# A new instruction list for the first half of a fused conv and gMLP kernel, with normalizations allowed on GpSimd

## The chip, the core and the metric

The kernel runs on one core of one Trainium2 chip. The metric is device microseconds of one execution. A core has five engines with a queue of instructions each, which run in order: PE (TensorE, matmuls and transposes by identity), DVE (VectorE), ACT (ScalarE), POOL (GpSimd), and SP (SyncE), which here only issues transfers. They wait for each other by semaphores. PE's results land in PSUM, and DVE and ACT read them from there.

## What is computed

With S = 2048 positions and D = 640 channels, in bfloat16:

```python
sa, ca, ga, sb, cb, gb = split(silu(c) @ w_mod, 6)
h = layernorm(x) * (1 + ca) + sa
kv = shift_conv(k, 4 taps) * v                      # (S, D)
y = irfft(rfft(pad(kv)) * rfft(pad(ssm_k)))[:S] + kv * ssm_D   # long convolution along S
x = x + ga * (h * y)
h = layernorm(x) * (1 + cb) + sb
z = gelu(h @ w_in)                                  # (S, 2 * 864)
z1, z2 = z[:, :864], layernorm(z[:, 864:])
x = x + gb * ((z1 * (w_sp @ z2 + b_sp)) @ w_out)
```

## The kernel before

The channels are cut into 5 units of 128, the positions into 16 tiles of 128. A group is 4 tiles.

**Convolution, for each unit.** SP loads k and v transposed (line L513), PE forms the four taps with diagonal matrices (`taps`), DVE multiplies by v (`tv`, L545), the product goes to a scratch in HBM (`kvw`, L551) and is read back in the layout of the Fourier step (`ldX`, L382, which also loads ssm_k, `X<-in_A_ssm_k`). PE makes stage 1 of the transform (`s1`), ACT or DVE copies it to SBUF (`s1c`, L240). Then, for 8 pairs of frequencies, PE finishes the transform (`fwd`), ACT copies that of ssm_k (`khc`), DVE multiplies the two (`prod`, L454), POOL or DVE sums real and imaginary parts (`csum`, L468), PE transforms back (`inv`), ACT or DVE copies the result into Z (`zc`, L240). A unit's Z is turned by a DMA transpose (`zt`, ZT<-Z, L675; for the last unit on PE, `zfl`, with copies `zk`), PE makes the last stage (`y`, for the last unit `yl`), and DVE multiplies by the modulated h (`ym`, L668; `yml`, L730). ZT has one buffer: a unit's transpose can start only when the last `y` of the unit before has read it.

**First layernorm.** `ln1` takes the statistics of a tile of x, `rstd1` and `nmr1` give 1/sigma and -mean/sigma for 8 tiles, `xn` (L595 to L603) writes the normalized tile to gh, `ghm` (L651) multiplies and adds ca and sa. The vectors come from matmuls with w_mod, whose six parts are loaded by `ldw` (L610) through one buffer.

**Second half.** `res` (L688) adds to x, `ln2` and `ag2` take statistics, `rstd2` and `nmr2` follow, `zx` (L819 to L831) normalizes a tile. Group 0 goes in two pieces of two tiles and is turned on PE (`hfl`) and modulated out of PSUM (`hmod`, L851 and L853); groups 1 to 3 are turned by DMA (`turn`, L871) and modulated in place (`hmod2`, L873 to L880). PE multiplies by w_in (`zz`), ACT applies gelu. Up to here the order of all engines is a list written out, ORDER: each entry is an engine's letter (P, A, D, G for POOL, S) and the number of a recorded operation; the letter decides which engine does it, where the operation allows more than one, and the sequence decides the order on every engine. `fill` operations are matmuls on the identity whose result nobody reads; FILLS says how many matmuls each has. They stand in the list like the rest.

**Last part.** The mixing with w_sp (L964), the projection (L985) and the output follow in plain loops; the list doesn't reach them.

An operation names the engines that may do it, as here the first normalization:

```python
op("DA", "xn", fn, r=[("xt", (u, n)) for u in range(NU)] + [("mv1", n), ("rs1", n // 8)],
   w=[("gh", (u, n // TB)) for u in range(NU)])
```

Of the kernel before, what the change touches and what calls it, by code (L numbers as in the profile page):

```python
# [10 lines left out]
ALU = mybir.AluOpType  # L11
# [13 lines left out]
NU = 5  # L25
# [5 lines left out]
PE_FLIPS = (4,)  # L31
TB = 4
NQ = DU // 4
FILLS = (7, 2, 1, 1, 4, 3, )
MODE = ('susussus', 'susussus', 'susussus', 'susussus', 'susussus')
SLOTS = dict(Tf=2, W=2, X=3, X1=4, KH=9, T=3, Z=3, ZT=1, wm=1, big=2, dg=2, st1=2, s1=1, sm=2, pu=2, pz=2)
PSUM_TAGS = ("s1", "sm", "pu", "pz")


ORDER = """  # L40
S82 G101 A4 D0 D13 D14 A16 D100 A1 D15 D102 D109 D110 A111 D121 G5 D17 S2 G6 P1029 P8 A11 D86 A112 P1030 P7 S19 S21
P145 P148 D115 D10 D116 A118 A149 A146 A147 D23 P1031 P26 A150 A117 D18 G119 S83 D87 P1032 P151 P154 D103 P24 D122
A123 A124 G125 D27 A152 D104 G126 D25 G120 S20 A156 A106 A105 G107 G108 G113 G114 D153 S88 D90 S22 P28 D29 P30 A155
P227 A228 D31 A33 P142 D143 P167 A168 P171 A172 P139 S523 D527 P229 A230 D528 P157 S34 S32 S35 A158 G144 D140 P161
A162 P231 A232 P133 P159 A160 P169 A170 D134 P233 P136 D127 P163 A128 S84 A164 G36 S85 P165 D529 A166 G48 D530 P37
A137 D38 D129 P173 A174 D175 P176 G135 P41 A178 D177 G138 D42 A234 P179 A180 A181 P182 D183 P43 D44 S524 G141 P39 D40
A184 P185 G72 A531 A532 P195 D186 D196 S3 P9 A12 A533 P191 D192 S46 S47 P51 G187 P201 D202 D52 G188 P189 P193 A190
G197 G198 A534 A194 P211 D212 G213 P217 P199 P53 D218 P221 D222 S45 A200 P49 S526 A542 A543 S89 P205 G214 D206 G207
P203 G208 P245 A246 D54 P251 D252 D50 P215 S565 P55 D56 A544 P247 A248 P253 A254 P237 G130 G131 P568 A238 P566 A567
P249 A250 D216 P257 A258 D535 G60 S525 D204 P209 A210 D538 D539 D540 P235 S91 A236 P219 P255 A256 P241 A242 P239 G536  # L50
A240 G223 G224 P225 D93 P301 A569 D537 D541 D302 P259 D260 A545 G261 P291 D292 S570 P573 D574 P303 P571 D546 P265 A304
D266 S57 A220 A553 D549 P307 A308 S58 D572 S92 P243 A244 A226 D550 G262 P263 P65 P305 A306 G547 D548 P285 D286 P293
D551 P275 D276 G287 G288 A264 A557 P325 A326 D554 A294 P267 S59 D552 G707 G591 D612 D66 A558 P269 D270 G271 G272 P327
A328 P315 P289 A316 P63 D64 A559 P329 A330 S575 P576 D561 P309 D577 S94 P295 D296 A310 D96 A268 P578 P331 A332 P323
A324 S70 S71 D562 A563 G613 P273 D560 G595 P313 P375 D649 D579 P333 D334 A314 P67 A564 D68 G297 G298 A274 P61 D62 P319
G597 A376 A320 G598 D596 P349 D350 P77 A290 P377 A378 P343 D344 P73 P317 A555 D592 D556 D593 P379 A318 S599 P311 A312
P299 S69 G335 A380 G336 A300 P321 A322 G345 G346 P337 A338 P279 D78 P381 A382 D594 P600 G672 D74 D280 G281 D601 P79
P369 D370 P277 A278 P347 A348 P387 A388 D282 D80 P602 P383 A384 P283 D603 A284 S95 P399 A400 P604 D650 D605 G616 D617
P365 P359 P351 A352 P606 D366 D607 G371 G372 D360 G709 P401 A402 S97 D99 P395 A396 D676 P75 P403 A404 P353 D354 P385
A386 D614 D76 G655 P373 P405 G618 D619 A406 G361 G362 P363 P397 A398 S580 G355 P339 A374 P449 A450 P407 P367 A368 A364  # L60
D340 P413 P453 A454 D408 G615 D414 S620 P621 D622 P393 G609 A394 P341 A342 P451 A452 S81 D656 S98 P623 P391 A392 P439
G608 D651 G356 P357 D677 D624 P455 A358 P625 G652 A456 P389 A390 D440 P427 D626 G409 G410 P627 P411 D674 P417 P473
A474 D428 G429 A412 G430 P457 A458 D418 S657 G419 D420 P415 P433 D434 A416 P479 A480 P443 P421 A422 P471 A472 D444
P475 G653 G654 A476 P431 G435 D436 P461 A462 P423 D628 D424 P477 P437 A432 P658 D659 A478 G673 P467 A468 G629 D630
D631 P463 A464 P581 A582 G445 G446 P660 D661 G634 P481 D482 A438 P441 A442 P662 D663 P497 D498 P425 A426 P517 D518
P447 A448 G483 G484 D710 P465 A466 P664 P485 A486 D632 P507 D508 G713 P459 A460 P499 P469 G519 A470 D633 P487 G670
D665 S583 D488 A500 G520 P521 A522 P501 G509 G510 G675 P584 D502 P513 D514 G671 P511 P491 D492 G503 G504 A512 G493
A585 D494 G708 P489 A490 P515 A516 S678 P679 P505 A506 D680 P681 D682 G667 P495 G666 P683 D638 D684 A496 P719 D720
P721 A722 P685 D686 D687 P717 G692 D690 P715 D716 S586 P587 D691 A718 G639 D689 P723 D688 A588 D724 D725 D727 D726
D756 P589 A590 D755 P732 D728 D729 P746 D636 D731 G757 D758 A759 D760 D730 D733 D769 D768 G770 P1033 P1034 P761 D763  # L70
D765 D764 D734 D735 D738 G610 P762 A767 A766 P739 D736 D737 D771 S754 P809 P813 D635 P815 A810 S753 P781 A772 A773
A814 D637 P775 A779 D693 D831 G714 D695 D747 G711 G712 D696 A816 D833 D694 D832 A780 D834 D697 G835 D611 P774 D776
D777 D778 A782 D836 D837 D839 D838 P791 A792 D793 A840 D740 P811 A812 D644 D741 D742 D744 P788 A789 D643 P795 P805
A806 D668 D701 A796 D699 D642 P802 D700 P798 A799 A803 D641 S841 P784 D846 P821 A822 A785 P819 A820 A842 D844 P817
P823 A824 D845 D843 P877 D743 D745 D900 A878 P847 A848 P881 D640 A882 P889 A890 P850 D646 P864 A818 D698 D897 D898
D899 D786 G901 D902 D903 A906 D905 D904 A851 S907 P854 A855 D748 D751 D849 P887 D647 D749 D852 G702 D669 D706 D705
D783 A865 D703 P871 A888 P883 A884 D645 D963 D965 A872 D750 P875 A876 D648 A909 D752 P857 A858 P879 D704 A880 D964
A911 D910 P885 A886 D912 D966 D908 D807 G967 D968 P868 A869 D873 P861 A862 A969 D971 A970 D870 D972 P923 P913 A924
A914 P920 A921 P951 A952 P927 S973 D859 D797 D790 D922 P930 D794 A931 D932 D800 D915 A928 D801 P937 A938 D977 D976
A978 P947 A948 P916 P934 A917 A935 D975 P943 A944 D804 D974 P989 P996 P979 A997 A990 D929 D933 D808 D863 D787 G825  # L80
D826 A827 A980 D830 D829 D866 D867 D853 P1000 A1001 D918 P1003 A1004 D856 P1015 A1016 D919 P945 D874 D860 P982 A983
D1002 A946 D828 P1021 G891 D892 A893 D981 D991 D939 P993 D936 A994 A1022 D940 P986 D895 D1005 D925 D926 D896 A987
P1017 P1011 A1012 P953 A954 A1018 P1007 D984 D988 D992 D985 G957 D998 D894 A1008 P941 D1006 D958 A959 D961 A942 P1013
D995 A1014 P949 A950 D999 G1023 P1009 D1024 A1028 A1026 P955 A962 A956 P1019 D1025 D960 D1027 A132 A1020 A1010
"""


# [36 lines left out]
def kernel(  # L124
# [20 lines left out]
    nc = tc.nc  # L145
# [26 lines left out]
    xt = persist.tile([P, NT, D], BF16)  # L172
# [17 lines left out]
    mv2 = persist.tile([P, NT, ADIM], F32)  # L190
    rstd2 = persist.tile([P, NT], F32)
    nmr2 = persist.tile([P, NT], F32)
# [11 lines left out]
    with ExitStack() as actx:  # L204
        consta = actx.enter_context(tc.tile_pool(name="consta", bufs=1))
        gh = consta.tile([P, NT, D], BF16)
# [10 lines left out]
        mv1 = consta.tile([P, NT, ADIM], F32)  # L217
        rstd1 = consta.tile([P, NT], F32)
        nmr1 = consta.tile([P, NT], F32)
# [8 lines left out]
        op = plan.op  # L228
# [366 lines left out]
        def xn(n):  # L595
            def fn(e):
                if e is nc.scalar:
                    e.activation(gh[:, n, :], xt[:, n, :], ACT.Identity, bias=nmr1[:, n:n + 1], scale=rstd1[:, n:n + 1])
                else:
                    e.tensor_scalar(gh[:, n, :], xt[:, n, :], mv1[:, n, 0:1], rstd1[:, n:n + 1],  # L600
                                    op0=ALU.subtract, op1=ALU.mult)
            op("DA", "xn", fn, r=[("xt", (u, n)) for u in range(NU)] + [("mv1", n), ("rs1", n // 8)],
               w=[("gh", (u, n // TB)) for u in range(NU)])  # L603

        def mod(j):
# [205 lines left out]
        def norm_piece(g, p, ns, xn2):  # L811
# [7 lines left out]
            for i, n in enumerate(ns):  # L819
                first = i == 0 and p == 0  # L820

                def norm(e, n=n, first=first):
                    if first:
                        new(xn2, "Z", [P, TB, D])
                    dst = tl[xn2][:, n % TB, :]
                    if e is nc.scalar:
                        e.activation(dst, xt[:, n, :], ACT.Identity, bias=nmr2[:, n:n + 1], scale=rstd2[:, n:n + 1])  # L827
                    else:
                        e.tensor_scalar(dst, xt[:, n, :], mv2[:, n, 0:1], rstd2[:, n:n + 1], op0=ALU.subtract, op1=ALU.mult)
                op("DA", "zx", norm, r=[("mv2", n), ("rs2", (g, p)), ("nm2", (g, p))] + [("xt", (u, n)) for u in range(NU)] + ([] if first else [(xn2, "new")]),  # L830
                   w=[(xn2, n % TB)] + ([(xn2, "new")] if first else []), new=[(xn2, "Z")] if first else [])  # L831

        def flip_piece(g, p, ns, xn2, hT):
# [24 lines left out]
        def z_group(g):  # L858
# [9 lines left out]
            if g >= PE_GROUPS:  # L868
# [4 lines left out]
                for dt in range(ND):  # L873
# [3 lines left out]
                            e.activation(h, h, ACT.Identity, bias=sb_col[:, dt:dt + 1], scale=cb1_col[:, dt:dt + 1])  # L877
                        else:
                            e.tensor_scalar(h, h, cb1_col[:, dt:dt + 1], sb_col[:, dt:dt + 1], op0=ALU.mult, op1=ALU.add)
                    op("DA", "hmod2", modulate, r=["sb", "cb"], w=[(hT, (dt, 0))])  # L880
            def p_of(n):
                return [n in q for q in pieces(g)].index(True)
            tags = ("pu", "pz", "pu", "pz")
# [156 lines left out]
```

## Time and profile before

| | us |
|---|---|
| median of 6 runs | 320.87 |
| lowest and highest run | 319.0, 321.86 |
| the profiled execution, its own time | 320.26 |
| its span, first to last instruction | 318.5 |
| PE busy | 306.8 |
| DVE busy | 208.5 |
| ACT busy | 152.4 |
| POOL busy | 104.1 |

How to read it: the profile has one row for each instruction with its start and duration; groups of rows give a line of the kernel, engine, operation, tile written and tiles read, shape, count, total and mean duration, and then the engine's idle time in front of them with what ended it. In the 40 slices a digit is the busy share of a slice of 8 us in tenths. The first 16 or 17 slices are the part up to the matmuls with w_in; after it DVE, ACT and POOL have little to do. The chain of waits is followed back from the last instruction, at each step to what released it.

### The profile page before, as it was taken

The numbers are of one execution on the slowest core, as the hardware profiler recorded it, in microseconds if no ns is written. First come the engines' busy times: TensorE is split into PE (matmuls) and PEld (weight loads), VectorE is DVE, ScalarE is ACT, GpSimd is POOL, SyncE is SP. The second block draws the span as 40 slices with busy tenths as digits, with TensorE's granted clock in tenths as the row PEclk, the third lists the DMA queues.
The fourth block names the chain that finished last, engine by engine and source line by source line (L and its number), as shares of the span: only waits on it lengthen the run. The fifth ranks groups of instructions, "written<-read, shape, count | busy, mean of one in ns | idle before, by whom it ended". The sixth has DMA issues, their size and how long they took to land.

```text
span 318.5 us, 6389 instructions
## 1 busy us (share of the span) xinstructions
PE 306.8 (96%) x2574; PEld 203.2 (64%) x2574; DVE 208.5 (65%) x448; ACT 152.4 (48%) x270; POOL 104.1 (33%) x134
## 2 busy tenths in 40 slices
PE   7988999999999998999999999999999999999996
PEld 2666787877899897555555555555555555555554
DVE  7899999989899899998957961522222223332333
ACT  4989899998798655676777682000000000000001
POOL 2665464878688897722001120000000000000000
PEclk9999999999999999999999999999999999999999
DMA  8999999996966398030429307896556555522221
GB/s 148 248 241 249 247 261 252 226 218 173 239 168 134 106 201 315 2 65 18 84 56 169 59 1 166 195 214 93 141 115 118 115 115 117 115 51 49 49 51 62
DMA packets 127026, 45.00 MB, mean 141 GB/s; under 512 B 116144, under 2 KB 126229, under 8 KB 126997
## 3 DMA queue, kind: packets, MB, share of 16 engines
q1 hardware_dynamic: 126698, 44.29, 63.3%
q8 instruction: 20, 0.33, 0.4%
q10 hardware_dynamic: 298, 0.31, 0.3%
q14 instruction: 10, 0.07, 0.1%
HBM read 16.11 MB, written 5.24 MB: 67 GB/s over the span
## 4 chain that ended last, share of the span: by engine, by line
PE 75%; DMA 13%; DVE 5%; SPq 4%; POOL 1%; issue 1%; ACT 1%; DVEq 0%; POOLq 0%
PE ps L964 29%; PE pu L237 13%; PE pz L237 13%; PE po L985 9%; PE sm L237 6%; DMA X<-kv_scr 4%; DMA kv_scr<-big 4%; SPq L513 3%; PE s L237 3%; DMA ZT<-Z 3%; DMA wm<-in_w_mod_dram 2%; DVE Tf L454 2%; POOL W L468 1%; ACT Z L827 1%; SPq L382 1%
## 5 line engine op out<-in xcount | busy, mean ns | idle before, releaser
L964 PE MATMUL ps<-X,wT 128*128 128x432 bf16 x512 | 95.7, 346 | 0.0
L964 PEld LDWEIGHTS <-wT 128*128 128x128 bf16 x512 | 50.1, 98 | 42.2
L977 ACT COPY uT<-pt 128x896 bf16<-128x896 bf16 x1 | 0.9, 906 | 118.4 <-PE pt L976 118.4
L237 PEld LDWEIGHTS <-Z 128*128 128x128 bf16 x320 | 31.2, 98 | 26.9 <-DVE Z L853 0.3
L237 PE MATMUL pu<-X,M 128*128 128x128 bf16 (+1 forms) x480 | 45.3, 237 | 1.0 <-DVE Tf L454 0.9
L237 PEld LDWEIGHTS <-M 128*128 128x128 bf16 x480 | 37.2, 98 | 5.8 <-issue 1.3
L468 POOL TENSOR_TENSOR W<-Tf 128x256 bf16<-128x256 f32 x46 | 33.8, 756 | 18.9 <-DVE Tf L454 17.0
L967 DVE SCALAR_TENSOR_TENSOR u<-ps,bcol,G 128x432 bf16<-128x432 f32 x18 | 12.0, 667 | 42.3 <-PE ps L964 42.3
L985 PE MATMUL po<-w_o,uT 128*128 128x320 bf16 (+2 forms) x231 | 33.2, 295 | 0.1
L240 ACT CAST X<-s 128x1024 bf16<-128x1024 f32 x30 | 30.9, 1030 | 4.1 <-PE s L237 3.7
L237 PE MATMUL pu<-big,Z 128*128 128x432 bf16 x160 | 32.6, 346 | 0.0
L237 PE MATMUL pz<-big,Z 128*128 128x432 bf16 x160 | 32.3, 346 | 0.0
L454 DVE TENSOR_TENSOR Tf<-pu,KH 128x1024 f32<-128x1024 f32 x25 | 30.2, 1218 | 2.6 <-PE pu L237 1.4
L967 DVE SCALAR_TENSOR_TENSOR u<-ps,bcol,M 128x432 bf16<-128x432 f32 x14 | 9.3, 667 | 31.6 <-PE ps L964 31.6
L985 PEld LDWEIGHTS <-uT 128*128 128x128 bf16 (+1 forms) x231 | 22.2, 97 | 9.9 <-issue 0.2
L237 PEld LDWEIGHTS <-G 128*128 128x128 bf16 x330 | 24.9, 98 | 1.6
L240 ACT CAST Z<-pz 128x512 bf16<-128x512 f32 x38 | 22.4, 601 | 7.1 <-PE pz L237 7.0
L240 ACT CAST KH<-pu 128x512 bf16<-128x512 f32 x40 | 23.4, 602 | 2.4 <-PE pu L237 2.4
L987 DVE TENSOR_TENSOR ot<-po,xt 128x320 bf16<-128x320 f32 (+1 forms) x33 | 15.9, 482 | 12.6 <-PE po L985 12.6
L237 PEld LDWEIGHTS <-X 128*128 128x128 bf16 x288 | 17.9, 97 | 7.5 <-DMA X<-kv_scr 3.3
L237 PE MATMUL s<-F1bd,X 128*128 128x256 bf16 x128 | 19.2, 272 | 1.5 <-DMA X<-kv_scr 1.3
L237 PE MATMUL sm<-big,dg 128*128 128x512 bf16 (+1 forms) x80 | 20.1, 379 | 0.5 <-DVE dg L530 0.3
(146 smaller groups left out, 417.2 us busy)
## 6 DMA issues: line engine op xcount, KB each, us to landing
wm<-in_w_mod_dram SPq DMA_DIRECT2D x6, 800.0 KB, 5.9
xt<-in_A_q_dram SPq DMA_DIRECT2D x4, 640.0 KB, 6.4
out_dram<-ot SPq DMA_DIRECT2D x15, 160.0 KB, 2.4
big<-in_B_w_in_dram SPq DMA_DIRECT2D x2, 1080.0 KB, 9.7
X<-in_A_ssm_k_dram SPq DMA_DIRECT2D x4, 512.0 KB, 6.2
kv_scr<-big SPq DMA_DIRECT2D x4, 512.0 KB, 4.3
X<-kv_scr SPq DMA_DIRECT2D x4, 512.0 KB, 4.3
w_o<-in_B_w_out_dram SPq DMA_DIRECT2D x6, 160.0 KB, 4.5
```

What stands on the lines that cost most here:

```text
L237: nc.tensor.matmul(o, lhsT=w, rhs=x, start=start, stop=stop)
L240: (e.copy if e is nc.scalar else e.tensor_copy)(dst, src)
L382: e.dma_start(tl[name][:, cs, :], src[:, d0 // 8 + cs.start:d0 // 8 + cs.stop, :])
L454: e.tensor_tensor(T_[:], (tl[pu] if src is None else tl[src])[:, :, :, None, :].to_broadcast(shape), tl[KH][:, :, None, :, :].to_broadcast ...
L468: e.tensor_tensor(tl[W][:, :, o, :], T_[:, :, 0, o, :], T_[:, :, 1, 1 - o, :], op=ALU.add if o else ALU.subtract)
L513: e.dma_start_transpose(tl[name][:, o + h * m:o + (h + 1) * m], src[0, h * m:(h + 1) * m, dt * P:(dt + 1) * P])
L827: e.activation(dst, xt[:, n, :], ACT.Identity, bias=nmr2[:, n:n + 1], scale=rstd2[:, n:n + 1])
L964: nc.tensor.matmul(ps[:, :FC], lhsT=wTs[t][:, s_, :], rhs=tl["z2_%d" % (s_ // TB)][:, s_ % TB, fc * FC:(fc + 1) * FC], start=(s_ == 0), st ...
L967: nc.vector.scalar_tensor_tensor(u[:, sl], ps[:, :FC], bcol[:, t:t + 1], z1[t][:, sl], op0=ALU.add, op1=ALU.mult)
L977: nc.scalar.copy(uTs[t][:], pt[:])
L985: nc.tensor.matmul(ps[:, :hi - lo], lhsT=uTs[t][:fsz[ft], ft, :], rhs=w_o[:fsz[ft], ft, lo:hi], start=(ft == 0), stop=(ft == NFT - 1))
L987: nc.vector.tensor_tensor(ot[:, lo:hi], ps[:, :hi - lo], xt[:, t, lo:hi], op=ALU.add)
```

## The change

The list is replaced by another one, with 1032 entries instead of 1035 (three fills fewer). `xn`, `zx` and `hmod2` may also stand on POOL, and on POOL the two normalizations are written as x * rstd + (-mean * rstd) in place of (x - mean) * rstd. Nothing else differs. The diff without the list itself:

```diff
-FILLS = (7, 2, 1, 1, 4, 3, )
+FILLS = (9, 2, 3, )
...
 def xn(n):
...
+                elif e is nc.gpsimd:
+                    e.tensor_scalar(gh[:, n, :], xt[:, n, :], rstd1[:, n:n + 1], nmr1[:, n:n + 1], op0=ALU.mult, op1=ALU.add)
                 else:
                     e.tensor_scalar(gh[:, n, :], xt[:, n, :], mv1[:, n, 0:1], rstd1[:, n:n + 1],
                                     op0=ALU.subtract, op1=ALU.mult)
-            op("DA", "xn", fn, ...
+            op("DAG", "xn", fn, ...
...
+                    elif e is nc.gpsimd:
+                        e.tensor_scalar(dst, xt[:, n, :], rstd2[:, n:n + 1], nmr2[:, n:n + 1], op0=ALU.mult, op1=ALU.add)
...
-                op("DA", "zx", norm, ...
+                op("DAG", "zx", norm, ...
...
-                    op("DA", "hmod2", modulate, ...
+                    op("DAG", "hmod2", modulate, ...
```

The first entries of the list, before and after (0 is the identity, 82 the first load, 101 an iota, 4 a table load, 18 and 13 bits of the partition number, 100 steps of the angles):

```diff
-S82 G101 A4 D0 D13 D14 A16 D100 A1 D15 D102 D109 D110 A111 D121 G5 D17 S2 G6 P1029 P8 A11 D86 A112 P1030 P7 S19 S21
+D0 D18 D100 A4 D13 A1 S82 G101 D102 D109 D15 D110 A111 A112 D115 G5 S2 D6 D14 A16 P1029 P8 D11 D86 P7 A10 A23 D17
```

Operations by engine where the lists differ in number:

| operation | before | after |
|---|---|---|
| xn, 16 | DVE 9, ACT 7 | DVE 2, ACT 3, POOL 11 |
| zx, 16 | DVE 9, ACT 7 | DVE 8, ACT 3, POOL 5 |
| hmod2, 15 | DVE 11, ACT 4 | DVE 4, ACT 3, POOL 8 |
| s1c, 48 | DVE 6, ACT 42 | DVE 9, ACT 39 |
| zc, 40 | DVE 2, ACT 38 | DVE 4, ACT 36 |
| zn (second layernorm of z), 16 | DVE 10, ACT 6 | DVE 12, ACT 4 |
| csum, 50 | DVE 4, POOL 46 | DVE 7, POOL 43 |
| diag (the taps' diagonals), 5 | DVE 1, POOL 4 | ACT 1, POOL 4 |
| kvw, 6 | SP 5, ACT 1 | SP 4, ACT 2 |
| ldw, 6 | SP 6 | SP 5, ACT 1 |

`ghm` (24 on POOL, 16 on DVE) and `res` (10 and 11) keep their numbers, but not the same tiles. Order of SP's transfers between the third and the last kv write (kvw 2 is unit 2's; XK is ssm_k's X, XU that of kv; k and v are the transposing loads):

```
before: w_mod 1, kvw 2, k 3, XU 2, v 3, w_mod 2, XK 3, k 4, v 4, ZT 0, kvw 3, XU 3, XK 4, w_mod 3, ZT 1, kvw 4, XU 4, ZT 2, w_mod 4
after:  kvw 2, w_mod 1, k 3, XU 2, v 3, w_mod 2, k 4, XK 3, v 4, ZT 0, XK 4, XU 3, ZT 1, kvw 4, XU 4, ZT 2, w_mod 4
```

In the list after, kvw 3 and w_mod 3 stand on ACT.

## The prediction

> **What bounds the kernel now.** I read the page first: busy times, the 40 slices, the chain.
>
> ```profile
> PE 306.8 (96%) x2574; PEld 203.2 (64%) x2574; DVE 208.5 (65%) x448; ACT 152.4 (48%) x270; POOL 104.1 (33%) x134
> ...
> DVE  7899999989899899998957961522222223332333
> ...
> PEclk9999999999999999999999999999999999999999
> ```
>
> PE is nearly always busy and its clock is full, but a busy PE is not a PE at its peak. So I took the start-to-start time of each kind of PE work where it runs unhindered: six matmuls of 1024 columns 0.44 us, taps 0.86, five gelu-input matmuls 0.91. From the first gelu-input matmul (131.25 us in the timeline) PE has 58.9 us of such work left and ends it at 190.9, so it loses 0.7 us there; from there to 318.5 it never stops. In front of 131.25 it has 116.1 us of work, so 15.2 us are lost. Only those, and the fill matmuls, can be gained.
>
> DVE is the other side. In front of the last modulation that the first gelu-input matmul needs (L853, starting at 131.13) stand 133.0 us of DVE instructions; they start within 2 us of their sum because neighbours overlap by some 0.04 us. Between them are 21 gaps of over 0.15 us, 8.4 us together: DVE is full but for these. Nearly all end at a PE instruction. The chain says where PE's delay comes from:
>
> ```profile
> 70.18 0.76 DVE Tf L454
> 70.93 4.32 DMA kv_scr<-big
> 75.30 4.28 DMA X<-kv_scr
> 79.63 0.61 PE s L237 x4
> ...
> 95.92 8.38 DMA ZT<-Z
> 104.34 0.41 PE sm L237 x8
> ```
>
> A kv write, its read back and a transpose of Z each sit between a DVE step and a PE step. PE's losses by the waits that end at a transfer: 1.3 us at 21.9, 0.7 at 37.9, 0.6 at 48.9 (w_mod), 0.9 at 78.8, 0.9 at 103.5.
>
> **Part one, work moved between engines.** The rows used:
>
> ```profile
> L600 DVE TENSOR_SCALAR gh<-xt,mv,rstd 128x640 bf16<-128x640 bf16 x9 | 4.1, 473 | 0.0
> L345 POOL TENSOR_SCALAR M<-M,sgn 128x512 bf16<-128x512 bf16 x4 | 3.0, 752 | 5.4 <-ACT M L340 5.4
> L367 POOL TENSOR_SCALAR G<-G 128x1024 bf16<-128x1024 bf16 x4 | 4.1, 1047 | 2.7 <-ACT G L240 2.6
> L651 POOL TENSOR_TENSOR gh<-gh,gca_bf 128x512 bf16<-128x512 bf16 x13 | 15.5, 1204 | 1.7 <-ACT X L240 1.1 <-DVE gh L600 0.7
> L240 DVE CAST X<-s 128x1024 bf16<-128x1024 f32 x2 | 2.5, 1225 | 1.1 <-PE s L237 1.1
> L240 DVE CAST X<-pz 128x512 bf16<-128x512 f32 x2 | 1.4, 684 | 0.0
> ```
>
> DVE, ahead of that modulation: normalizations xn, 9 become 2 (one of the nine took 0.75, the rest 0.44): -3.4. Stage-1 copies, 6 become 9: out 4 x 0.68 + 2 x 1.22, in 5 x 0.68 + 4 x 1.22: +3.1. Two more copies of pz into Z, 0.68 each: +1.4. Three more sums (L468), 0.45 to 0.63: +1.0. One residual and one bn_stats more, one L651 and one L829 less, diagonal and sk copy gone, two tiny copies come: -0.6. Sum +1.6 (unrounded). DVE is not relieved but loaded: by its load alone the switch comes 1.6 us later.
>
> GpSimd gets 11 xn at L600's new branch, 5 of zx, 8 of hmod2. Its one-input price for 640 elements is not in the trace: at least 0.62 (512 elements, L349), at most 1.5 (L651 scaled by 640/512); between L345 (0.75 at 512) and L367 (1.05 at 1024) I take 0.85. It starts the first xn when nmr1 is there, about 39 us. Eight xn and seven other steps later the sums for one product (op 262) end at 51.5, and PE wants them at 52.3: the cover is 0.8 us. At 0.95 it is used up; at 1.5 PE waits 4.4 us there. ACT loses 11 us of work and was idle half the time: zero; its new kv writes and w_mod load block only copies that run ahead.
>
> A rule speaks against this move. The Trainium skill (GPSIMD Engine Reference, Key points) says that GpSimd shares its SBUF interfaces with VectorE and contends with DVE instructions of two SBUF inputs or in a 2-port mode. The trace has it mildly: one L600 took 0.75 instead of 0.44, one L688 1.17 instead of 0.41, while GpSimd ran; such cases cost DVE some 2 us over 104 us of GpSimd work, so 16 us more GpSimd work cost 0.3 us. The page has no figure for it; by the trace the sum changes by 0.3 at most, which I leave in the range.
>
> **Part two, the fills.** Eighteen become fourteen. The first group grows from 7 to 9, at 0.45 each +0.9 us; it hides behind the F1 table, which DVE now reaches after 5.9 us of work instead of 4.4 and which then holds PE until 7.4 (before 6.2). That hides in turn, since the first kv read comes at 23. The seven fills at 127.95 covered a wait for the normalization; gone, they leave an idle PE of about 2 us. No PE idle that long is in the trace, and all 40 slices show the full clock; I take zero, at most what half rate cost at the start (0.45 against 0.22 us a matmul, so 3 us if it lasted 6). The Trainium skill (TensorE: Matmul & The Clock Gate, What's actually happening) halves the clock after an idle window of about 3.4 us; by it 2 us is safe, and a 3.4 us gap would cost an estimated 1.7. "Identity first" moves nothing: it already stands first on DVE.
>
> **Part three, the order.** For each DVE step that reads PE's output I took DVE's work ahead of it less PE's work up to the end of its producer: its lead. The larger, the more delay PE may have before DVE waits. Smallest leads, before and after, by DVE's work ahead: at 24 to 32 us 7.5 and 9.1; 40 to 48: 10.2 and 11.5; 56 to 64: 11.3 and 13.0; 72 to 80: 12.3 and 14.5; 104 to 112: 13.3 and 14.9; 120 to 128: 14.4 and 16.0. PE's delay before (start less own work ahead) is 7.3 at 23 us, 9.2 at 38, 10.2 at 55, 11.3 at 80, 12.6 at 105: it ran just at the leads, hence the 8.4 us.
>
> PE's delay after, transfer by transfer with the durations of before. First kv read: both halves are written by 15.4 where SP again stood behind a transpose (15.1 before), 7.1. Second: last kv product at 28.5, SP free at 29.2 as before, 9.3. Second part of w_mod: the wait of 0.6 goes, since PE has 1.3 us more ahead of it. The load of ssm_k for unit 3 (X<-in_A_ssm_k) is moved on SP behind the transposes of the last k, which took 7.1 us:
>
> ```profile
> 55.44 0.52 SPq L382 DMA_DIRECT2D X<-in_A_ssm_k_dram  x1
> 56.01 7.08 SPq L513 DMA_TRANSPOSE big<-in_A_k_dram  x1
> ```
>
> It then issues at 62.5 and lands 4.5 to 6.2 later; DVE's addD (71.4 us of work ahead; without gaps the overlap grows by 0.08 us per us, since from 13 to 131 us DVE won 1.9 us on its sum in spite of 7.8 us of gaps, so 4.5 by then) is there at 67, so DVE waits 0 to 1.8 and PE's delay becomes 9.6 to 11.5. The read of kv for unit 3 lands at 78 against PE's 79.3: its 0.9 goes. The ZT chains have 0.4 to 1.1 us more PE work between the transpose's release and its reader: 0.9 goes, small rest. Delay at 105: 10.3 to 11.5, and DVE may run 16.0 ahead: it starts its steps 4.5 to 5.7 us earlier than its own work ahead (1.3 before), and 0.5 more at the end. So the last modulation starts at 134.6 - 5.0 = 129.6 to 134.6 - 6.2 = 128.4, against 131.13: 1.5 to 2.7 earlier, middle 2.1. The load of part one is in it.
>
> Behind that, 58.9 us of PE work stand in both lists. The second piece's two normalizations now sit on GpSimd (0.85 instead of ACT's 0.91) behind two residuals, ready at 132.6, wanted at 133.6: zero, with 1 us of cover. hmod2 on three engines is ready 1 us before PE; later groups have more.
>
> Sum: span 318.5 - 2.1 = 316.4; the profiled execution has 1.8 outside its span, 318.2; it lay 0.6 under the median of the runs, so 318.8.
>
> **Rivals.** (1) No change: the leads are spent by PE delays I don't see, about 2 us more at the late ssm_k load or by contention; the 1.6 us of load remains and waits balance it. For it: DVE was at 93%. Against: all leads grew. 319.3 to 322.4, likeliest 320.7. (2) Slower: GpSimd becomes the bound at the first normalizations. It decides above 0.95 us per xn; at 1.5 PE waits 4.4 us at 52. Of that up to 2.2 would come later anyway at the ssm_k load, and the second half's zx and hmod2 on GpSimd lose their 1 us of cover, 0.65 x 2: net loss 4.4 - 2.2 + 0.3 = 2.5 against a gain of 2.1, and each further contended DVE step adds to it; with 1.5 us of DVE slowing, 322.8. For it: L651's 1.2 us. Against: three one-input rows under 1.05. (3) The list doesn't do what it says: identity doesn't, the rest of the list does.
>
> **How the numbers follow.** Forecast 0.52, 318.8, own range 317 to 319.3. No change 0.28. Slower 0.20. 0.5% is 1.6 us, about what a measurement can tell here. Range 316.4 (all transfers early, 0.3 of further waits gone) to 322.6: this leaves about a tenth at each end.
>
> **What would show it.** Right: the PE waits for kv_scr at 79 and ZT at 104 are gone; DVE's gaps ahead of L853 sum to 4 to 6 us; the first gelu-input matmul starts at 128.5 to 129.7; xn on POOL 0.75 to 0.95 us. Wrong: W or gh on POOL releasing PE around 50, X<-in_A_ssm_k releasing DVE for over 2 us at 67 to 72, a clock below 1 at 128, or PE waits behind 131.

## The result and the profile after

The changed kernel is slower: 322.46 us in the median of 30 runs (319.68 to 328.1), against 320.19 us of 65 runs of the kernel before (319.0 to 323.67). The ratio is 1.0048 with a 95% interval of 1.0032 to 1.0065. Ratios leave out the runs that lie over 1.5% above their kernel's fastest (8 of these 30, 7 of them with a low clock) and medians do not, so the ratio understates what the clock costs. The profiled execution took 321.19 us, 0.9 more than that of before and 1.3 under the median of its runs; its span is 319.3. The page of the changed kernel, busy times and slices:

```profile
PE 306.9 (96%) x2570; PEld 203.4 (64%) x2570; DVE 210.8 (66%) x443; ACT 143.5 (45%) x259; POOL 120.6 (38%) x153
...
DVE  8999999997999999987658773522222223333333
...
PEclk9999999999999999999999999999999999999999
```

DVE has 2.3 us more to do, GpSimd 16.5 more, ACT 8.9 less, and DVE's slices up to the seventeenth are as full as before or fuller, but for the tenth. The clock is full in this execution, but not in every run of the changed kernel: the runs list a mean clock each, and it is below 0.997 in 14 of the 30. PE's waits of the changed kernel from 0 to 145 us (line and what it waited for, us in total, times, longest), the costliest but for one at the start that both kernels have:

```profile
PE pz L237 <- DMA X<-kv_scr: 1.5, 1, 1.5
PE sm L237 <- DMA ZT<-Z: 1.2, 1, 1.2
PE s L844 <- ACT Z L829: 1.1, 1, 1.1
PE sm L237 <- DMA big<-in_A_k_dram: 0.8, 1, 0.8
PE pu L237 <- ACT KH L240: 0.6, 1, 0.6
```

The same view of the kernel before has:

```profile
PE s L237 <- DMA X<-kv_scr: 1.3, 2, 0.7
PE pz L237 <- DMA X<-kv_scr: 1.2, 1, 1.2
PE sm L237 <- DMA ZT<-Z: 0.7, 1, 0.7
PE sm L237 <- DMA wm<-in_w_mod_dram: 0.4, 1, 0.4
```

The first wait of the changed kernel is for the first kv read (1.2 before). The second is at the first transpose of Z, at 77 us; before, the wait for ZT was at 104. The third is the wait in front of `hfl` at 131 us, where the seven fills were. The last two, for a load of k and for ACT's copy KH of the transform of ssm_k, are new. PE waited 3.6 us for transfers, and waits 3.5 now. The waits have changed places, not gone. The chain of the changed kernel:

```profile
66.50 10.54 DMA ZT<-Z
77.09 0.41 PE sm L237 x8
...
97.39 8.32 DMA ZT<-Z
```

Of the links that the prediction showed, the kv write and read at 70 to 80 us are gone, and a transpose of Z that takes 10.54 us stands there; the later one is as long as before (8.38). Step by step in the timelines:

| start of | before | after |
|---|---|---|
| PE on the first kv read | 22.98 | 24.02 |
| PE on the second kv read | 38.52 | 39.03 |
| PE on the first transpose of Z | 74.29 | 77.09 |
| PE on the kv read of unit 3 | 79.63 | 81.96 |
| PE on the third transpose of Z | 104.34 | 105.76 |
| the last modulation (L853 before) | 131.13 | 132.27 |
| the first gelu-input matmul | 131.25 | 132.39 |
| end of the list's PE work | 190.89 | 191.68 |

The loss of about 1 us is there at the first kv read, and never falls below a half of that. These are single profiles, and the first read moves from one to the next: it starts at 22.94 to 24.00 us in three whose list is that of before up to there (before, e7, e8), at 23.48 to 24.42 in five that share the changed list up to there (after, e2, e3, e5, e6). So the 1 us is likely, but not sure, to come from the list.

### The profile page after: what moved, and what is told of

It reads as the page before. It is cut to its first block, busy times and chain, and to the rows that moved or that the text cites. A ratio compares the mean times of both kernels' runs of the same rounds, so it can differ in the third digit from the quotient of the medians.

```text
span 319.3 us, 6384 instructions
## 1 busy us (share of the span) xinstructions
PE 306.9 (96%) x2570; PEld 203.4 (64%) x2570; DVE 210.8 (66%) x443; ACT 143.5 (45%) x259; POOL 120.6 (38%) x153
## 4 chain that ended last, share of the span: by engine, by line
PE 75%; DMA 9%; DVE 9%; SPq 2%; ACT 2%; issue 1%; POOL 0%; DVEq 0%
PE ps L968 29%; PE pu L237 16%; PE pz L237 14%; PE po L989 9%; DMA ZT<-Z 6%; PE sm L237 4%; PE s L237 3%; DMA xt<-in_A_q_dram 2%; SPq L513 2%; DVE X L240 1%; DMA X<-in_A_ssm_k_dram 1%; DVE Tf L454 1%; DVE big L545 1%; DVE st L572 1%; PE pu L711 1%
## 5 line engine op out<-in xcount | busy, mean ns | idle before, releaser
L237 PEld LDWEIGHTS <-Z 128*128 128x128 bf16 x320 | 31.2, 98 | 26.9 <-DVE Z L857 0.3
L237 PE MATMUL pu<-X,M 128*128 128x128 bf16 (+1 forms) x480 | 46.1, 237 | 0.9 <-ACT KH L240 0.6
L468 POOL TENSOR_TENSOR W<-Tf 128x256 bf16<-128x256 f32 x43 | 31.5, 755 | 12.6 <-DVE Tf L454 12.5
L240 ACT CAST X<-s 128x1024 bf16<-128x1024 f32 x28 | 28.8, 1030 | 3.7 <-PE s L237 3.1
L240 ACT CAST Z<-pz 128x512 bf16<-128x512 f32 x36 | 21.1, 598 | 5.1 <-PE pz L237 5.0
L912 DVE BATCH_NORM_STATS2 stz<-X 128x6 f32<-128x432 bf16 x32 | 18.2, 587 | 4.6 <-ACT X L906 4.6
```

Source lines behind the costliest of these rows:

```text
L237: nc.tensor.matmul(o, lhsT=w, rhs=x, start=start, stop=stop)
L240: (e.copy if e is nc.scalar else e.tensor_copy)(dst, src)
L468: e.tensor_tensor(tl[W][:, :, o, :], T_[:, :, 0, o, :], T_[:, :, 1, 1 - o, :], op=ALU.add if o else ALU.subtract)
L912: op("D", "stz", lambda e, i=i, n=n, fc=fc: e.bn_stats(out=stz[:, n, fc, :], in_=tl[z2][:, i, fc * FC:(fc + 1) * FC]), r=[(z2, (i, fc))], ...
```

## The experiments

Four causes were tried. Expectations call them S (lost in the first 28 us, at the first kv read), L or D (DVE's load, and DVE instructions that run longer beside GpSimd), T (transfers that end last) and C (fills and clock). "Full clock" counts runs with a mean clock of 0.997 or more. DVE is its busy time ahead of the last modulation and, behind the slash, its idle time there; both come from the one profiled run, which in e3 (327.66 us) and e9 (328.23) lies well above the median. In kernels whose list is one line shorter every line number below it is one less.

| kernel | median | ratio to before, 95% | full clock | DVE busy / idle |
|---|---|---|---|---|
| before | 320.19 | 1 | 125 of 141 | 133.0 / 9.7 |
| after | 322.46 | 1.0048 [1.0032, 1.0065] | 16 of 30 | 138.1 / 6.3 |
| e1_kvw_act | 321.05 | 1.0010 [0.9977, 1.0042] | 5 of 12 | 137.9 / 4.5 |
| e2_kvw3_sp | 324.89 | 1.0141 [1.0087, 1.0195] | 1 of 6 | 138.9 / 10.2 |
| e3_tail_fills | 322.80 | 1.0073 [1.0039, 1.0107] | 10 of 12 | 139.0 / 11.5 |
| e4_copies_act | 323.36 | 1.0099 [1.0067, 1.0130] | 6 of 9 | 131.8 / 13.6 |
| e5_kload_late | 326.94 | 1.0138 [1.0095, 1.0181] | 0 of 6 | 137.9 / 13.0 |
| e6_xn_back | 323.70 | 1.0062 [1.0039, 1.0085] | 6 of 12 | 141.2 / 5.7 |
| e7_before_xn_pool | 325.50 | 1.0129 [1.0089, 1.0170] | 1 of 6 | 131.9 / 14.5 |
| e8_before_no_tail_fills | 322.75 | 1.0037 [1.0012, 1.0062] | 0 of 12 | 133.1 / 12.2 |
| e9_masks | 324.61 | 1.0072 [1.0039, 1.0104] | 3 of 12 | 136.9 / 12.6 |
| e10_kv0_act | 324.17 | 1.0060 [1.0026, 1.0093] | 2 of 12 | 135.9 / 10.4 |
| e11_kvw_tail | 321.91 | 1.0003 [0.9977, 1.0030] | 11 of 12 | 138.2 / 7.7 |
| e12_all | 322.02 | 1.0017 [0.9990, 1.0043] | 11 of 12 | 136.3 / 9.8 |
| e13_z0_transfers | 325.39 | 1.0076 [1.0042, 1.0110] | 2 of 12 | 138.1 / 8.5 |
| e14_z0_kvw_fill | 322.06 | 0.9974 [0.9935, 1.0013] | 6 of 12 | 138.2 / 4.4 |
| e15_before_kvw | 323.42 | 1.0044 [1.0017, 1.0071] | 5 of 12 | 132.6 / 13.8 |
| e16_e14_stats_later | 320.88 | 0.9993 [0.9967, 1.0019] | 11 of 12 | 138.2 / 6.3 |
| e17_z0_kvw_seven | 324.25 | 1.0083 [1.0052, 1.0115] | 4 of 11 | 139.0 / 6.7 |
| e18_z0_kvw_early | 320.21 | 0.9979 [0.9952, 1.0006] | 12 of 12 | 138.4 / 4.8 |

The kernel before ran beside each group and had 320.26 (e1 to e4), 321.66 (e5 to e8), 321.82 (e9 to e12), 321.34 (e13 to e16) and 320.97 (e17, e18): compare ratios, not medians, across groups. The full clock of the first row counts these 141 runs.

### The fills and the clock

e8, the kernel before without its seven late fills, and e3, the changed kernel with them:

```diff
 e8  -FILLS = (7, 2, 1, 1, 4, 3, )     +FILLS = (7, 2, 1, 1, )
     -G770 P1033 P1034 P761            +G770 P761
 e3  -FILLS = (9, 2, 3, )              +FILLS = (9, 2, 3, 4, 3, )
     -G692 P761                        +G692 P1032 P1033 P761
```

> The kernel before without its seven fill matmuls at 127.95 us (FILLS 7, 2, 1, 1), nothing else changed. Theory C (these fills kept the clock): the clock is below 0.997 in a third of the runs or more (1 of 26 in the kernel before), with half clock within 5 us behind 128, and the median rises by 0.5 to 1 us to 320.8 to 321.3. The forecast's price for them (zero): the median stays at 320.2 within 0.3 and the clock at 1.0. Theories T and D: as the forecast.

> The list after, with the two fill groups of 4 and 3 matmuls put back in front of the first transposes of the normalized x (hfl), where the list before had them. Theory C (PE's idle 1 us at 130 lets the clock fall in some runs, which read 0.984 to 0.995 and were up to 6 us longer): every run reads a clock of 1.000 and the median falls by 1 us or more. Theories S and L: the fills only fill a wait; the median stays within 0.4 us, and the low clocks, if they are made at the start of the kernel, stay as frequent.

e8 shows what the fills are worth where they stood: at most 0.37%, 1.2 us, and no run of twelve has the full clock. The timeline of PE in e8 shows why:

```profile
129.06 1.75 PE L236 MATMUL pz<-Ebd,X 128*128 128x16 bf16 x64
132.53 0.51 PE L843 MATMUL s<-ident,Z 128*128 128x128 bf16 x6 [1.72 <-ACT Z L828]
...
133.93 3.42 PE L236 MATMUL pu<-big,Z 128*128 128x432 bf16 x10
```

After an idle time of 1.72 us the first ten gelu-input matmuls take 3.42 us. In the kernel before, behind the seven fills, the same ten took 2.15:

```profile
127.95 1.89 PE L237 MATMUL s<-ident 128*128 128x512 bf16 x7
129.89 0.49 PE L840 MATMUL s<-ident,Z 128*128 128x128 bf16 x6
...
131.25 2.15 PE L237 MATMUL pu<-big,Z 128*128 128x432 bf16 x10
```

The granted clock of e8 is 0.5 from 133.45 to 136.87. Not all of the 1.2 us is this place, though: in the profiled run the clock is also halved from 24.23 to 27.64, behind a wait of 2.49 us for the first kv read, where the list is still that of before. Two such stretches make its mean clock of 0.988. Five of the twelve runs have 0.988 or 0.989; the other seven, with 0.993 to 0.995, have a median of 322.60, 0.95 us above the full-clock runs of the kernel before beside them (321.65). So an estimate for the late stretch alone is 1 us.

In the changed list fills at this place bring the full clock back (10 of 12 in e3, and 11 of 12 in e11), but not the time: from the first `yl` to the first `hfl` PE needs 5.7 us in e3 and in e11, and 5.0 in the changed kernel. There the wait is only 1.1 us, shorter than the seven fills that should cover it (1.9 us in the kernel before).

e17 and e18 have the same transfers (below) and differ in their fills alone:

```diff
 e17 +P1032 (4 matmuls) P1033 (3) ahead of P761, the first mixing transpose
 e18 +P1032 (5 matmuls) ahead of P173, PE's first work on the first kv read; P1033 (5) ahead of P761
```

> The changed kernel with the order of the Z transfers of before, the second half of unit 0's kv write on ACT, and seven fills (not three) ahead of the first mixing transpose. With three fills the clock was full in 6 of 12 runs and those had 319.6 us, 0.995 of the kernel before at full clock. Theory C (low clocks come from the wait at 128 to 134): full clock in 10 of 12 runs or more, and the fills' own 0.7 to 0.9 us: 0.996 to 0.998 of the kernel before. If the low clocks come from the first kv read's wait at 21 to 24 us: still low in a third of the runs or more, 0.999 to 1.002.

> The same, but with five fills in the wait for the first kv read (PE idle from 21.4 to 24 us, where a half-clock stretch begins at 22 to 25.6 us in four of the profiled runs) and five ahead of the first mixing transpose. If both waits let the clock fall: full clock in 11 of 12 runs, 0.994 to 0.997. If only the late one does: as with seven fills there, 0.996 to 0.998. If five late fills are too few: clock low in a third of the runs, 0.998 to 1.001.

They ran side by side, and 1% lies between them. PE's timeline in e17, which has seven late fills and no early ones:

```profile
...
22.67 1.04 PE L236 MATMUL sm<-big,dg 128*128 128x512 bf16 x4 [2.24 <-DMA big<-in_A_k_dram]
23.55 1.84 PE L236 MATMUL pu<-X,M 128*128 128x256 bf16 x12
25.18 1.91 PE L236 MATMUL sm<-big,dg 128*128 128x512 bf16 x4
26.88 0.46 PE L236 MATMUL pz<-F1bd,X 128*128 128x256 bf16 x2
```

and in e18:

```profile
21.90 1.05 PE L236 MATMUL pu<-X,M 128*128 128x256 bf16 x12
22.79 1.02 PE L236 MATMUL sm<-big,dg 128*128 128x512 bf16 x4
23.65 1.24 PE L236 MATMUL s<-ident 128*128 128x512 bf16 x5
25.00 0.39 PE L236 MATMUL pz<-F1bd,X 128*128 128x256 bf16 x2
```

In e17 PE idles 2.24 us in front of taps, for the load of k, and from 23.62 us on, at half clock, twelve matmuls take 1.84 us and four taps 1.91, which take 1.05 and 1.02 in e18. So the clock falls not only at the late wait but also at the waits of 20 to 25 us, for the first kv read (e8) or for the load of k beside it (e17), and seven late fills cannot help there. This part of theory C is shown. It falls at still other waits: at 54.2 us in e7, at 80.92 in e3, behind 2.1 us of waiting for the first transpose of Z.

That the early fills are the cure is likely, but not shown. The counts speak for it, 12 of 12 runs at full clock against 4 of 11. But the five matmuls on `ident` in e18, the early fills, stand behind the taps: they cover the wait for the kv read, and cannot cover the wait for k that started e17's stretch. That wait is missing from e18's profile, although the two lists are the same up to the fills, so part of the 1% may be the transfers of that run. e18's ratio lies below the changed kernel's with intervals apart; that it beats the kernel before is likely (0.9979), not certain.

### DVE and GpSimd

```diff
 e4  -D226 D268 D358 D416 D228 D232 D254     +A226 A268 ... (four copies into Z and three of stage 1 go to ACT)
 e6  -G549 ... G562 (the eleven xn)          +D or A, as in the list before
 e7  the list before, -D or A549 ... 562     +G549 ... G562
 e9  -D127 ahead of D42                      +D127 behind D184, at 30.5 us
```

> The list after, with the copies of stage 1 of ops 228, 232 and 254 and the copies of Z of ops 226, 268, 358 and 416 on ACT, as before, instead of DVE: 3 x 1.22 + 4 x 0.68 = 6.4 us less on DVE, 3 x 1.03 + 4 x 0.60 = 5.5 us more on ACT, which is idle for 34 us of that part. Theory L: DVE's steps come up to 6 us earlier until PE's leads bind, the first gelu-input matmul at 129 to 131 instead of 132.4, 1.5 to 3 us less. Theory S: the part behind 28 us is bound by the chain through PE and the transfers, at most 0.5 us less.

> The changed kernel with the eleven normalizations xn on the engines that they had before (eight on DVE, three on ACT), all else as changed: the one part undone. Theory D: DVE's instructions ahead of the first gelu-input matmul lose about 1.5 of the 3.8 us by which they run over their kind's fastest, but carry 8 x 0.44 = 3.5 us more, so DVE has some 2 us more to do and, if it is the bound, the median is 323.5 to 325. If contention costs more than the load relieved, the median falls below the changed kernel's 322.5, to 321 or so. Theory T: PE waits for transfers decide, DVE has slack there: 322 to 323 and the same wait of 1.3 us at the first transpose of Z.

> The changed kernel with one step moved: the three small mask instructions of DVE (L303 to L305, 1.01, 0.97 and 1.09 us beside GpSimd, where two of them take 0.2 alone) stand five DVE steps later, at 26 to 28 us, where GpSimd is idle. Only what runs beside what changes. Theory D (DVE, slowed by GpSimd, is the bound): they take 1.4 us together instead of 3.0, DVE's busy time ahead of the last modulation falls from 138.1 to 136.5, and the median falls by 1 to 1.5 us to 1.000 to 1.002 of the kernel before. Theory T (PE's waits for transfers set the time; after relieving DVE in one kernel and loading it in another neither moved with its load): the DVE time falls the same but the median stays at 1.004 to 1.006.

> The kernel before, its list unchanged but for the eleven normalizations xn, which go to GpSimd: the one part alone. By the forecast's own prices (0.85 us each on GpSimd, 3.5 us off DVE, 0.3 us of contention): 318.3 to 319.3. Theory D: the DVE instructions run 1 to 2 us longer beside GpSimd, and GpSimd's sums and multiplications come later: 319.8 to 321, no gain. Theory T: the read of kv and the transposes of Z end last wherever DVE stands: 320.0 to 320.5. If GpSimd becomes the bound (W or gh of GpSimd releasing PE at 50 to 75 us): 321.5 to 323.

DVE's load does not set the time. e6 adds 3.1 us to it, 1% of the time, and is the same as the changed kernel within its interval. e4 takes 6.3 us away and is slower (1.0099): DVE's idle time grows by 7.3. e4 by itself proves little, since its seven copies went to ACT, and in its profile PE waits 6.1 us for ACT up to 145 us, where the changed kernel waits 2.6 (for the copy KH alone 1.9 against 0.6). e9 changes nothing but what runs beside three small mask instructions. The timeline of DVE in the changed kernel:

```profile
20.73 1.01 DVE L303 TENSOR_SCALAR e2i<-fidx,ek,er 128x16 int32<-128x16 f32 x1
21.77 0.97 DVE L304 TENSOR_SCALAR e2i<-e2i 128x16 int32<-128x16 int32 x1
22.66 1.09 DVE L305 TENSOR_SCALAR cmask<-fidx,pnum 128x4 f32<-128x4 f32 x1
```

and their groups in e9 (lines one less; the last two numbers ahead of the bar's idle time are us in total and mean ns):

```profile
L302 DVE TENSOR_SCALAR e2i<-fidx,ek,er 128x16 int32<-128x16 f32 x1 | 0.3, 296 | 0.0
L304 DVE TENSOR_SCALAR cmask<-fidx,pnum 128x4 f32<-128x4 f32 x1 | 0.2, 224 | 0.0
L303 DVE TENSOR_SCALAR e2i<-e2i 128x16 int32<-128x16 int32 x1 | 0.2, 175 | 0.0
```

3.07 us become 0.70 where GpSimd is idle, a larger gain than I expected (to 1.4), and the time does not fall: 1.0072 with 3 of 12 runs at full clock. e12 and e11 repeat it with steady clocks: DVE 1.9 us less busy, idle 2.1 us more, 1.0017 against 1.0003, where a bound DVE would have given 0.6% back. By this pair and e6 theory D falls as the cause.

e7 shows what the rest of the changed list is needed for. In the list before, `xn` on GpSimd costs 1.3%. The chain of e7:

```profile
49.70 0.73 POOL W L468
50.43 2.61 POOL gh L600 x3
53.04 0.70 POOL W L468
...
53.79 0.66 PE pz L237 x6
```

Three normalizations stand between two sums that PE waits for, 1.8 us here and 2.5 us a second time, and at 54.2 us the clock halves. That is the mechanism of my second rival; the changed list puts the sums ahead, and its longest wait for a sum is 0.3 us.

### The transfers

```diff
 e1  -S34 ... S33 S35 (SP)           +A114 A33 (ACT issues the second half of unit 0's kv write)
 e10 e1, and -S84 ... S85            +A172 A84 A85 (and its two reads)
 e11 e1 and the fills of e3
 e12 e11 and the masks of e9
 e15 the list before, -S34 S32 S35   +A155 P227 A32 A228
 e2  -A69 ahead of P375              +S599 S69 (kv write of unit 3 on SP behind the first Z transpose)
 e5  -S97 D99 ahead of S95           +S95 S97 ... D605 D99 (ssm_k of unit 4 behind the kv read of unit 3)
 e13 e2, and S97 behind S95, D99 behind D614
 e14 e13 and e1 and 3 fills ahead of P761
 e16 e14, -A542 A543 A544            +A246 A542, A204 A543, A242 A544 (statistics behind PE's copies)
 e17, e18: e13 and e1 and the fills shown above
```

> The list after, with one entry moved: the second half of unit 0's kv write (kvw, op 33) is issued by ACT behind its mneg (op 114) instead of by SP behind the transposes of the next k. Theory S (the loss is made in the first 28 us, at the first read of kv, which came at 24.0 instead of 23.0, and everything behind follows it): the read comes about 1 us earlier, the first gelu-input matmul at 131.4 instead of 132.4, the time 0.8 to 1.1 us below that of the list after. Theory L (DVE's added load and its instructions lengthened beside GpSimd are what lost the gain; the start only shifts waits): the read earlier, the first gelu-input matmul within 0.4 us of 132.4. Theory C (the clock, see the fills): no change of the spread of the runs.

> The list after, with unit 3's kv write moved from ACT's queue (69.5 us, beside the transpose of Z of unit 0) to SP's behind that transpose, as it stood before. If the transpose took 10.5 us instead of 8.4 because the write ran beside it from a second queue, ZT 0 lands about 2 us earlier and PE's wait of 1.3 us at 75.3 and DVE's of 1.25 us at 77.5 go; if the load of X behind it on SP is the cause, it stays. Theory S: the time stays within 0.5 us, since DVE finds other waits. Theory L: up to 1.2 us less.

> The changed kernel, in which the ssm_k load for unit 4 (issued at 71.5 us, beside the first transpose of Z) is moved on SP behind the read of kv for unit 3, and its DVE user behind it. Theory T (the loss comes from transfers that run beside the first transpose of Z, 10.5 us where it took 8.4 before, and the PE wait of 1.3 us behind it also starts half-clock stretches): the transpose's chain falls to 8.5 to 9.2 us, the PE wait at 75 to 78 us to 0.3 or less, fewer than a quarter of the runs have a clock below 0.997 (14 of 30 in the changed kernel), median 321.0 to 321.5, 1.003 of the kernel before. Theory D (DVE instructions that run longer beside GpSimd make DVE the bound): DVE is untouched, 322.3 to 322.6. Theory C (the seven tail fills that are gone let the clock fall at 128 us): the clock is as often low as in the changed kernel, 322.5.

> The changed kernel with the transfers around the first transpose of Z in the order of before: kv write of unit 3 on SP behind that transpose (instead of on ACT beside it), then the read back, then the ssm_k load of unit 4 and, later, its DVE step. Theory T (the transpose takes 10.2 to 11.3 us in the changed list, 8.4 in the kernel before and 8.4 where only the kv write was moved back; PE waits 1.3 to 3 us for it): issue to first reader 8.4 to 8.9 us, no PE wait over 0.3 us at 75 to 86 us, the median falls by 1 to 1.5 us to 1.000 to 1.002 of the kernel before (half clock at 130 us stays in about half of the runs). If the kv read back then ends last instead: a PE wait of 1 to 3 us for X<-kv_scr at 80 to 85 and 1.005 to 1.010.

The transpose of Z: the last line of the view of the tile ZT gives the times from issue to landing of the kernel's four transposes, least, median and longest. e5, with the ssm_k load out of the way:

```profile
DMA to landing us min/median/max: 6.7/7.6/10.1
```

and e13, with the kv write on SP behind it:

```profile
DMA to landing us min/median/max: 6.7/7.9/8.4
```

So it is the kv write of unit 3, which the changed list issues from ACT at 69.48 us, 2.98 us behind the transpose, that goes with the 2 us, not the ssm_k load. It does so only when it comes early: in e1, e4 and e6 ACT issues the same write 3.95 to 5.74 us behind the transpose, no transpose takes over 8.5 us, and PE waits for Z for 0.2 us at most. But neither version gains. In e2, where the write alone was moved back, PE does not wait for Z but 2.7 us for the kv read at 85 us, and half clock follows from 85.84. e5 makes a wait of its own, 3.5 us, because the DVE step that reads this load (addD, X<-X,D_col), which I moved too, now waits for it in front of a sum that PE needs. In e13 PE waits for the other transfer instead, as the expectation allowed, in PE's timeline:

```profile
84.49 0.61 PE L236 MATMUL s<-F1bd,X 128*128 128x256 bf16 x4 [2.78 <-DMA X<-kv_scr]
```

> The changed kernel in which ACT's queue issues the second half of unit 0's kv write and both halves of its read back, so that neither stands behind the transposes on SP (the read was issued at 20.8 us, behind a transpose that ended at 20.5). Theory T: the read is issued at 19.3 to 19.8, PE's first matmul on it starts at 22.6 to 23.2 instead of 24.0, and the median falls by 0.8 to 1.2 us, to 1.001 to 1.002 of the kernel before. If the transfer itself slows by the same amount, as with the write alone on ACT: 24.0 again, 1.003 to 1.005. Theory D: the first 30 us are DVE's, no change, 1.005.

> The changed kernel with the second half of unit 0's kv write issued by ACT (1.001 alone, with half clock at 130 us in 7 of 12 runs) and the seven fills put back ahead of the first mixing transpose at 129 us. Theory C (without these fills the clock halves for 3.4 us at 130 to 134, some 1.2 us of time): runs below 0.997 fall to 2 of 12 or fewer, no half-clock stretch behind 128 us, and the ratio falls by 0.003 to 0.997 to 0.999. Without C: 1.001 as alone.

> The changed kernel with three edits together: the kv write's second half on ACT, the mask instructions later, the seven fills back. Theory D and C: 0.994 to 0.996 of the kernel before, since the masks add 1 us to what the write and the fills give. Theory T and C: 0.997 to 0.999, as without the masks.

> The kernel before with one edit: the other half of unit 0's kv write is issued by ACT at 13 us instead of by SP at 15.1 behind a transpose, so that SP issues the next transpose 0.6 us earlier. If this place is what cost the changed kernel its time (the same edit there: 1.001 without and 1.000 with fills, where it was 1.005 and 1.007), the first read starts earlier here too: 0.996 to 0.998. If it helps only in the changed list, whose later steps are tighter: 0.999 to 1.001.

With unit 0's write on ACT the changed list is at 1.0003 with fills (e3, the same fills without it, 1.0073; the intervals are apart). Yet PE's first work on that read does not start earlier in the profiles (24.5 in e1, 24.7 in e11), the reads on ACT as well (e10) lose, and in the list before the same edit costs 0.4%, with the first read at 25.2 us and half clock behind it. e11's profile even has a longer wait for Z (2.3 us) than the changed kernel's. By which path e11 gains is not shown.

> The same, with the second half of unit 0's kv write on ACT and three fills ahead of the first mixing transpose (seven kept the clock in 32 of 36 runs but took 0.7 to 0.9 us of PE where it waited 1.2). Theory T and C: 0.993 to 0.997 of the kernel before, clock at or over 0.997 in 8 of 12 runs or more. If three fills are too few for the clock: 0.998, clock low in half of the runs.

> The kernel with the order of the Z transfers, the kv write on ACT and three fills, and three bn-statistics passes of ACT (L568, the first waits for its x load until 37.4 us) moved behind the copies of k and Z that stand behind them on ACT and for which PE waits 0.75 us at 42. If ACT's own queue is one of the new waits: 0.3 to 0.7 us under the kernel without this edit, 0.991 to 0.995. If DVE or the transfers end last anyway: the same as without.

Both together, unit 0's write on ACT and unit 3's on SP, are in e14 and e16 to e18, and their worth is not settled. At full clock e14's six runs have a median of 319.62, against 321.12 of the kernel before beside it, 1.5 us faster; its other six have 323.2 to 327.0, and all twelve 322.06, against 321.34. But e17, with the same transfers and four more fills, has 322.21 in its four runs at full clock, against 320.73 beside it, and e18 320.21. Runs at full clock are also those in which the waits were short, so they may flatter e14. e16 is steady, but its statistics cost what they should bring: PE waits 1.4 us for ACT's copy KH.

## Why the prediction was wrong

**GpSimd's price, right.** `xn` on GpSimd was taken at 0.85 us, the group of the changed kernel:

```profile
L600 POOL TENSOR_SCALAR gh<-xt,rstd,nmr 128x640 bf16<-128x640 bf16 x11 | 9.8, 903 | 1.1 <-issue 0.8 <-DVE nmr L592 0.2
```

A mean of 0.90, within the 0.75 to 0.95 foretold, and no wait for it at 50 us.

**DVE's load, mis-sized, and not the bound.** Forecast +1.6 us, measured 138.1 - 133.0 = +5.1. The count was right (four copies of 1.22, five of 0.68, two xn left); what was missed is how much longer DVE instructions run: the masks 3.07 us instead of 1.40, the fifteen L653 7.6 where L651's mean would make them 6.6, the six L392 0.9 more. I had 0.3 for all of it. Beside the row, the Trainium skill (GPSIMD Engine Reference, Key points) does name the shared interface; that section gives no size, and the rows show one where a GpSimd instruction of 1 us runs: 0.2 us can become 1. Most of it comes from the new order of neighbours, not from xn, since with xn back (e6) the same 3 us remain: DVE has 3.1 us more, about the 3.5 counted for eight xn.

**DVE's gaps, right and without meaning.** They fell from 8.4 to 5.3 us (4 to 6 foretold). A step that failed here is to add load and gaps as if a shorter one left the other alone: from e11 to e12 the gaps took what the load gave, 2.1 us for 1.9.

**PE's delay by transfers "with the durations of before", wrong.** This is the step that failed first of all. The forecast had PE's delay at 105 us fall from 12.6 us to between 10.3 and 11.5. Instead PE is idle for 9.4 us ahead of the first gelu-input matmul, where it was for 8.5 (busy 123.0 of 132.39 us, and 122.8 of 131.25). The first read was put where it was, and came 1.0 us later in this profile: SP's last transposes ahead of it took 4.58 and 4.13 us (3.92 and 3.48 before), beside a kv write issued 2.4 us earlier. That the write is the reason is not shown, since in e8, with the write where it was, they took 5.19 and 3.88. The waits for w_mod and for unit 3's kv went, as foretold, and DVE did not wait for the late ssm_k load. But the first transpose of Z had no price for the write that ACT now issues beside it (I counted that write as ACT's work alone: zero): 10.54 us for 8.45, and a PE wait of 1.2 us. ACT's queue was taken at zero otherwise too; its copy KH, which stands behind a statistics pass and starts at 42.06 us, makes PE wait 0.6.

**The fills at zero, wrong.** Of the median's 2.3 us, 0.6 is the clock (321.83 in the 16 runs at full clock, 322.46 in all). e8 puts the price in the list before at 1.0 (estimate) to 1.2 us. I gave 2 us of idle PE no price because no such stretch was in the trace. The Trainium skill (TensorE: Matmul & The Clock Gate, What's actually happening) has the clock halve after an idle window of about 3.4 us. The length agrees with the half-clock stretches of the runs (3.41 us), but 1.0 to 2.7 us of idle PE were enough, so my "2 us is safe" is refuted.

**The sum.** Forecast -2.1 us. At full clock +1.6, and in the two profiles the first gelu-input matmul is 1.1 later. DVE's load, 3.5 more than counted, and the gaps that did fall come out near that as a sum, by luck: e6 and e12 show that DVE's load does not set the time. On PE's side 2.4 us of waits went (1.3 for later kv reads, 0.7 for ZT at 104, 0.4 for w_mod) and 2.9 came (0.3 at the first read, 1.2 at Z, 0.8 at the taps' k, 0.6 at KH), besides the 1.1 where the fills were. That these waits set the time is argued from this and from the DVE runs, not shown by undoing them: of the 1.6 us only unit 0's write moved the ratio clearly (e11 against e3), by a path that stays open. How much each wait adds to the end stays open as well, since single profiles differ by more (PE's first kv read starts at 23.5 to 26.9 us with the changed list and its variants).

**The rivals.** That waits would balance (no change) was nearest in mechanism, and 322.46 lies just above its 319.3 to 322.4. GpSimd as the bound happened only in e7. Of the signs of being wrong, the low clock near 128 us came: e1's, e6's and e10's profiles have it at 130.27 to 134.81.

## What to carry to other kernels

Where several engines trade waits, take away load on paper only after asking what refills the gap: here 6 us less on DVE, put on ACT, made the kernel slower, and 1.9 us less with nothing put elsewhere left it the same. Price a moved transfer by what runs beside it at its new time, not by its row at the old one, and give a removed fill the clock's price (here about 1 us) unless the wait it covered goes with it. A run list with the mean clock of each run shows a clock loss that one good profile hides.

## What the runs showed of the hardware

In all profiled runs the half-clock stretches before the end begin at whole multiples of 3.413 us (5, 6, 14, 22 to 24, 36 to 39) after the clock first rose, as at 17.07 us behind it in e17, 78.51 in e2 and 129.71 in e6, and last 3.41 us, or twice that (e5). The clock first rose at 4.6 to 7.5 us, so the same wait can fall differently on this grid from run to run. That would explain why only some runs of a kernel lose; only one run of each kernel was profiled, so it is not shown. Of the grid's windows up to 145 us, all eight in which PE was idle for 2.0 us or more (2.03 to 2.72) were followed by half clock; of those with 1.0 to 1.9 us eight were, six of them at 127 to 138 us, and others with up to 1.89 were not; why less was enough there was not tried.

Three DVE instructions of 0.2 to 0.3 us beside GpSimd instructions of 1.04 us took 0.97 to 1.09 us, each as if it ended with one of them. Not every DVE instruction does: in the same profile three of 0.10 to 0.21 us at 20.41 to 20.69 us ran beside GpSimd at their usual length.

The longest transpose of Z took 8.3 to 8.6 us in the ten profiled runs without a kv write from ACT's queue beside it, and 10.1 to 11.1 in the seven in which ACT issued that write of 512 KB to HBM 1.6 to 3.0 us behind it. In the three in which the write came 3.95 us or more behind, it took 8.3 to 8.5.
